# Spreading softmax reciprocals through a DRAM row, and loading q and k by block: an attention and MoE kernel on Trainium2

## Chip, cores and metric

The kernel runs on one core of a Trainium2 chip. The metric is the device time of one execution in microseconds (us). The kernel before took 657.95 us (median of 3 runs, 656.72 to 660.94). Kernels are compared only within the same rounds.

## The reference

A forgetting attention (batch 8, 8 heads, 576 positions, head size 64) feeds a two-layer MLP with SiLU ("MoE" in the kernel's names):

```python
cum    = np.cumsum(np.log(np.clip(f, 1e-4, 1.0)), axis=-1)
scores = q @ k.T / 8 + (cum[..., :, None] - cum[..., None, :])   # causal
attn   = softmax(scores)
x      = (attn @ v).transpose(0, 2, 1, 3).reshape(4608, 512)
h      = x @ w_in                      # 512 x 2048
out    = (h * sigmoid(h)) @ w_out      # 2048 x 512
```

All inputs and the output are float32. Matmuls may run in bfloat16.

## The kernel before

Two heads make a *pair* (32 pairs), one batch entry makes a *block* (4 pairs). TensorE's order is fixed by hand; the other engines' order is set by a scheduler. Softmax denominators (`den`) are formed for two pairs at once, so for four heads. I call that a *quad*; there are 16.

```python
    def load_pair(n):                       # SyncE, float32, 6 DMAs of 128 KB per pair
        b, p = divmod(n, NP)
        for name, src in (("q", q), ("k", k), ("v", v)):
            t = stage.tile([P, NM, 2, D], FP32, name=name + "f", tag=name + "f")
            for i in range(2):
                nc.sync.dma_start(out=t[:, :, i, :],
                    in_=src[b, 2 * p + i, 0:SM, :].rearrange("(c p) d -> p c d", p=P))
    # ... load_tails: the last 64 positions of all heads of a block
    # ... convert(n): GpSimd casts q and k to bfloat16 and scales v

    def den(qd):
        dn = psc.tile([P, 1024], FP32, name="dn", tag="sc")
        # ... for j in range(4), the heads of the quad:
                    nc.tensor.matmul(
                        dn[32 * j : 32 * j + 32, q0:q1],           # 32 equal rows per head
                        lhsT=w_bf[r, kb, bh : bh + 1].to_broadcast([nk, 32]),
                        rhs=rhs, start=..., stop=...)
        rec = recp.tile([P, S], FP32, name="rec", tag="rec")
        nc.vector.reciprocal(out=rec[:, :], in_=dn[:, 0:S])
        for m in range(2):
            rb = rbp.tile([P, S], FP32, name="rb", tag="rb")
            for i in range(2):
                j = 2 * m + i
                nc.sync.dma_start(                                  # one partition, 64 copies
                    out=rb[i * D : (i + 1) * D, :],
                    in_=rec[32 * j : 32 * j + 1, None, :].to_broadcast([1, D, S]))
            recs[2 * qd + m] = rb

    def num(n):
        # ... nm (PSUM) = numerator of the pair, 128 rows = 2 heads x 64
        rb = recs.pop(n)
        nc.vector.tensor_tensor(out=xT[:, p, b * S : (b + 1) * S],
            in0=nm[:, 0:S], in1=rb[:, :], op=ALU.mult)

    # main loop, per pair n: scores(n) and MoE work (fill); den(n//2 - 1) when n is even;
    # num(n-3), num(n-2) when n is odd; transposes(n+1)
```

`tp`, `sc`, `dn` and `nm` share one PSUM pool of two buffers. A `nm` tile is held until its xT multiply has read it, so a late `rb` holds PSUM, then the transposes, then the scores of the next pair.

The softmax here doesn't subtract the row's maximum and nothing guards it: scores larger than these inputs give would overflow.

Of the kernel before, what the change touches and what calls it, by code (L numbers as in the profile page):

```python
# [9 lines left out]
ALU = mybir.AluOpType  # L10
# [6 lines left out]
def kernel(  # L17
# [26 lines left out]
    ctx.enter_context(tc.manual_schedule(engines={mybir.EngineType.PE}))  # L44

    const = ctx.enter_context(tc.tile_pool(name="const", bufs=1))
    stage = ctx.enter_context(tc.tile_pool(name="stage", bufs=3))
    tailp = ctx.enter_context(tc.tile_pool(name="tailp", bufs=2))
    conv = ctx.enter_context(tc.tile_pool(name="conv", bufs=2))
    vpool = ctx.enter_context(tc.tile_pool(name="vpool", bufs=5))  # L50
    qktp = ctx.enter_context(tc.tile_pool(name="qktp", bufs=2))
    upool = ctx.enter_context(tc.tile_pool(name="upool", bufs=4))
    recp = ctx.enter_context(tc.tile_pool(name="recp", bufs=2))
# [1 line left out]
    gpool = ctx.enter_context(tc.tile_pool(name="gpool", bufs=2))  # L55
    tpool = ctx.enter_context(tc.tile_pool(name="tpool", bufs=3))
    opool = ctx.enter_context(tc.tile_pool(name="opool", bufs=2))
    psc = ctx.enter_context(tc.tile_pool(name="psc", bufs=2, space=bass.MemoryType.PSUM))
    pbig = ctx.enter_context(tc.tile_pool(name="pbig", bufs=4, space=bass.MemoryType.PSUM))


    stg: dict[int, tuple] = {}
    tails: dict[int, tuple] = {}

    def load_pair(n):
        b, p = divmod(n, NP)
        tiles = []
        for name, src in (("q", q), ("k", k), ("v", v)):
            t = stage.tile([P, NM, 2, D], FP32, name=name + "f", tag=name + "f")
            for i in range(2):  # L70
                nc.sync.dma_start(  # L71
                    out=t[:, :, i, :],
                    in_=src[b, 2 * p + i, 0:SM, :].rearrange("(c p) d -> p c d", p=P),
                )
            tiles.append(t)
        stg[n] = tuple(tiles)

    def load_tails(b):
        tiles = []
        for name, src in (("q", q), ("k", k)):  # L80
            t = tailp.tile([ST, H, D], FP32, name=name + "tf", tag=name + "tf")
            nc.sync.dma_start(
                out=t[:, :, :], in_=src[b, :, SM:S, :].rearrange("h s d -> s h d")
            )
            tiles.append(t)
        t = tailp.tile([P, NP, D], FP32, name="vtf", tag="vtf")
        for i in range(2):
            nc.sync.dma_start(
                out=t[i * ST : (i + 1) * ST, :, :],
                in_=v[b, i::2, SM:S, :].rearrange("h s d -> s h d"),  # L90
            )
        tiles.append(t)
        tails[b] = tuple(tiles)

    f_sb = const.tile([BH, S], FP32, name="f_sb")
    nc.sync.dma_start(out=f_sb[:, :], in_=f.rearrange("b h s -> (b h) s"))
    load_pair(0)
    load_tails(0)
    load_pair(1)
    load_pair(2)  # L100


    ident_bf = const.tile([P, P], BF16, name="ident_bf")
# [54 lines left out]
    nc.vector.tensor_copy(out=w_bf[:, :, :], in_=wps[:, :, :])  # L158


    qt_bf: dict[int, tuple] = {}
    qkT: dict[int, bass.AP] = {}
    vps: dict[int, bass.AP] = {}
    us: dict[int, tuple] = {}
    bf: dict[int, tuple] = {}

    def conv_tails(b):
        qt, kt, vt = tails.pop(b)
        qk_t = tailp.tile([ST, 2, H, D], BF16, name="qk_t", tag="qk_t")
        nc.gpsimd.tensor_copy(out=qk_t[:, 0, :, :], in_=qt[:, :, :])  # L170
        nc.gpsimd.tensor_copy(out=qk_t[:, 1, :, :], in_=kt[:, :, :])
        v_t = tailp.tile([P, NP, D], BF16, name="v_t", tag="v_t")
        for i in range(2):
            r = slice(i * ST, (i + 1) * ST)
            nc.gpsimd.tensor_tensor(
                out=v_t[r, :, :],
                in0=vt[r, :, :],
                in1=w_bf[r, NM, b * H + i : (b + 1) * H : 2, None].to_broadcast([ST, NP, D]),
                op=ALU.mult,
            )  # L180
        qt_bf[b] = (qk_t, v_t)

    def convert(n):
        b, p = divmod(n, NP)
        if p == 0:
            conv_tails(b)
        qf, kf, vf = stg.pop(n)
        qk_bf = conv.tile([P, 2, NM, 2 * D], BF16, name="qk_bf", tag="qk_bf")
        for i, t in enumerate((qf, kf)):
            nc.gpsimd.tensor_copy(  # L190
                out=qk_bf[:, i, :, :], in_=t[:, :, :, :].rearrange("p c h d -> p c (h d)")
            )
        vp = vpool.tile([P, NM, 2, D], BF16, name="vp", tag="vp")
        bh = b * H + 2 * p
        nc.gpsimd.tensor_tensor(  # L195
            out=vp[:, :, :, :],
            in0=vf[:, :, :, :],
            in1=w_bf[:, 0:NM, bh : bh + 2, None].to_broadcast([P, NM, 2, D]),
            op=ALU.mult,
        )  # L200
        bf[n] = qk_bf
        vps[n] = vp

    def transposes(n):
        b, p = divmod(n, NP)
        qk_bf = bf.pop(n)
        qk_t, _ = qt_bf[b]
        tp = psc.tile([P, 2, 1024], BF16, name="tp", tag="sc")
        for i in range(2):
            for c in range(NM):  # L210
                nc.tensor.transpose(  # L211
                    tp[:, i, c * P : (c + 1) * P], qk_bf[:, i, c, :], ident_bf[:, :]
                )
            nc.tensor.transpose(  # L214
                tp[:, i, SM:S],
                qk_t[:, i, 2 * p : 2 * p + 2, :].rearrange("p h d -> p (h d)"),
                ident_bf[:ST, :ST],
            )
        t = qktp.tile([P, 2, S], BF16, name="qkT", tag="qkT")
        nc.vector.tensor_copy(out=t[:, :, :], in_=tp[:, :, 0:S])  # L220
        qkT[n] = t
# [65 lines left out]
    def den(qd):  # L287
        dn = psc.tile([P, 1024], FP32, name="dn", tag="sc")
        for kb in range(NM + 1):
            for q0, q1 in q_parts(kb):  # L290
                for j in range(4):
                    n, i = 2 * qd + j // 2, j % 2
                    b, p = divmod(n, NP)
                    bh = b * H + 2 * p + i
                    u, ut = us[n]
                    r = slice(i * ST, (i + 1) * ST) if kb == NM else slice(0, P)
                    nk = ST if kb == NM else P
                    rhs = (
                        ut[r, :]
                        if kb == NM  # L300
                        else u[:, i, u_off(kb, q0) : u_off(kb, q0) + q1 - q0]
                    )
                    nc.tensor.matmul(  # L303
                        dn[32 * j : 32 * j + 32, q0:q1],
                        lhsT=w_bf[r, kb, bh : bh + 1].to_broadcast([nk, 32]),
                        rhs=rhs,
                        start=(kb == 0),
                        stop=(kb == NM or (kb == NM - 1 and q0 < SM)),
                    )
        rec = recp.tile([P, S], FP32, name="rec", tag="rec")  # L310
        nc.vector.reciprocal(out=rec[:, :], in_=dn[:, 0:S])  # L311
        for m in range(2):
            rb = rbp.tile([P, S], FP32, name="rb", tag="rb")
            for i in range(2):
                j = 2 * m + i
                nc.sync.dma_start(  # L316
                    out=rb[i * D : (i + 1) * D, :],
                    in_=rec[32 * j : 32 * j + 1, None, :].to_broadcast([1, D, S]),
                )
            recs[2 * qd + m] = rb  # L320

    def num(n):
        b, p = divmod(n, NP)
        u, ut = us.pop(n)
        vp = vps.pop(n)
        _, v_t = qt_bf[b]
        nm = psc.tile([P, 1024], FP32, name="nm", tag="sc")
        for kb in range(NM + 1):
            for q0, q1 in q_parts(kb):
                for i in range(2):  # L330
                    r = slice(i * ST, (i + 1) * ST)
                    nc.tensor.matmul(  # L332
                        nm[i * D : (i + 1) * D, q0:q1],
                        lhsT=v_t[r, p, :] if kb == NM else vp[:, kb, i, :],
                        rhs=(
                            ut[r, :]
                            if kb == NM
# [83 lines left out]
            ready["g"] += 1  # L421


    convert(0)
    transposes(0)
    for n in range(NU):
        scores(n, 0)
        fill(1)
        if n + 1 < NU:
            convert(n + 1)  # L430
        if n + 3 < NU:
            load_pair(n + 3)
            if (n + 3) % NP == 0:
                load_tails((n + 3) // NP)
        if n == 1:
            load_w_in(0)
        if n == 2:
            load_w_in(1)
        if n == 3:
            load_w_in(2)  # L440
            load_w_in(3)
        if 4 <= n < 8:
            load_w_out(n - 4)
        scores(n, 1)
        fill(1)
        scores(n, 2)
        fill(2)
        if n % 2 == 0 and n >= 2:
            den(n // 2 - 1)
            fill(2)  # L450
        if n % 2 == 1 and n >= 3:
            num(n - 3)
            fill(1)
            num(n - 2)
            finished(n - 2)
            fill(1)
        if n + 1 < NU:
            transposes(n + 1)
        fill(2)
# [38 lines left out]
```

## Time and profile before

| what | value | where it is read |
|---|---|---|
| span of the profiled run | 658.4 us | page |
| xT multiply waiting for rb | 233.6 us in 32 waits | list of waits |
| rb's DMAs on the chain that ended last | 39%, their issue 8% | page, chain |
| start of the second quad's last xT | 100.35 us | VectorE's timeline |
| 14 quads from there | 496.2 us, 35.4 us each | VectorE's timeline |
| rest (MoE alone) | 61.9 us | span less the two |

Lines of the page of the kernel before. A queue line gives packets, MB, and the time of its packets as a share of 16 engines' span; a group line gives busy us and mean ns, then idle time before the group and what ended it; the last line gives the median time from issue to landing. In all such lines PE is TensorE, DVE VectorE, ACT ScalarE, POOL GpSimd, SPq SyncE's queue, and L316 is line 316 of the kernel.

```profile
span 658.4 us, 7686 instructions
...
q1 hardware_dynamic: 124560, 47.35, 63.0%
...
DMA rb<-rec 39%; SPq L316 8%; PE po L389 8%; PE hp L362 8%; DVE rec L311 6%; ACT u L258 4%; SPq L71 2%; DMA kf<-in_k_dram 2%; DVE gt L371 1%; PE sc L251 1%; PE tp L211 1%; DVE xT L344 1%; DVE qkT L220 1%; DMA vf<-in_v_dram 1%; ACT th L370 1%
...
L344 DVE TENSOR_TENSOR xT<-nm,rb 128x576 bf16<-128x576 f32 x32 | 24.2, 758 | 233.6 <-DMA rb<-rec 233.6
...
rb<-rec SPq DMA_DIRECT2D x64, 144.0 KB, 14.1
```

VectorE waits 233.6 us, all for rb. That the wait matters, and is not just idle time of an engine with slack, shows in the chain in order of time (start, us, what), here one quad of the kernel before:

```profile
186.30 3.68 DVE rec L311
...
190.54 0.59 SPq L316
...
191.18 2.68 SPq L316
...
193.90 16.41 DMA rb<-rec
...
211.10 0.76 DVE qkT L220
...
217.17 1.83 PE po L389 x8
219.00 0.94 PE dn L303 x36
```

Reciprocal, four DMA issues, one long DMA, then qkT and some 7 us of TensorE work to the next den. The quantity that matters is the time from the reciprocal's end to the start of the quad's second xT. I call it **L2**. VectorE's timeline of the same quad gives it:

```profile
186.22 3.75 DVE L311 RECIPROCAL rec<-dn 128x576 f32<-128x576 f32 x1
191.02 0.75 DVE L220 COPY qkT<-tp 128x1152 bf16<-128x1152 bf16 x1
202.39 0.76 DVE L344 TENSOR_TENSOR xT<-nm,rb 128x576 bf16<-128x576 f32 x1 [4.15 <-DMA rb<-rec]
210.43 0.76 DVE L344 TENSOR_TENSOR xT<-nm,rb 128x576 bf16<-128x576 f32 x1 [6.69 <-DMA rb<-rec]
```

L2 is 210.43 - (186.22 + 3.75) = 20.5 us here.

The table of stretches has, for the tail of the kernel before, where only output rows move, the columns of PE, PEld, DVE, ACT and POOL busy time, then clock, DMA share and GB/s:

```profile
614.00:658.00 44.00, 40.56 (x188) 18.17 (x186) 11.49 (x17) 14.34 (x24) 0.00 (x0) 0.99 0.13 48
```

48 GB/s at a share of 0.13 of 16 engines is 48 / (0.13 x 16) = 23 GB/s for a busy engine.

### The profile page before, as it was taken

To read this page: it belongs to the slowest core of one execution; us is meant where nothing else is said; L and a number is where in the kernel's file an instruction comes from. 1 tells how busy PE (TensorE), PEld (TensorE's weight loads), DVE (VectorE), ACT (ScalarE), POOL (GpSimd) and SP (SyncE) were. 2 spreads that over 40 slices of the span, in tenths; PEclk is the share of its full clock that TensorE was granted. 3 is DMA by queue.
4 is the path that set the end of the run, shared out by engine and by line. 5 is a ranking of instruction groups with operands and counts; after the bars stand their busy time and mean duration, and the time that the engine had idled before them with its cause. 6 is when DMAs were issued, how large, how long until landed. Compare 5 with 4: busy or idle time off the path is not lost.

```text
span 658.4 us, 7686 instructions
## 1 busy us (share of the span) xinstructions
PE 428.6 (65%) x3013; PEld 184.5 (28%) x3013; DVE 230.1 (35%) x325; ACT 203.2 (31%) x312; POOL 99.0 (15%) x150
## 2 busy tenths in 40 slices
PE   3250428767385928775676838592877658907997
PEld 1130213323132413322232313231332224402443
DVE  2140405513272307340361317230643137304530
ACT  4130304422170405322442207140532235104441
POOL 6341202202011012101020201101110100000000
PEclk9999999979597978878795959687887969957999
DMA  8998787789867774868577674858382825592002
GB/s 174 211 207 42 128 32 143 27 147 88 132 69 74 120 72 95 33 130 49 124 40 108 50 110 47 66 96 46 96 31 33 35 40 18 36 32 52 16 33 80
DMA packets 128820, 52.03 MB, mean 79 GB/s; under 512 B 115920, under 2 KB 120016, under 8 KB 128784
## 3 DMA queue, kind: packets, MB, share of 16 engines
q1 hardware_dynamic: 124560, 47.35, 63.0%
q0 software_dynamic: 4224, 4.19, 4.0%
q8 instruction: 23, 0.38, 0.2%
q14 instruction: 13, 0.11, 0.0%
HBM read 36.85 MB, written 9.44 MB: 70 GB/s over the span
## 4 chain that ended last, share of the span: by engine, by line
DMA 42%; PE 20%; SPq 11%; DVE 11%; issue 10%; ACT 5%; POOL 0%; DVEq 0%; ACTq 0%; POOLq 0%
DMA rb<-rec 39%; SPq L316 8%; PE po L389 8%; PE hp L362 8%; DVE rec L311 6%; ACT u L258 4%; SPq L71 2%; DMA kf<-in_k_dram 2%; DVE gt L371 1%; PE sc L251 1%; PE tp L211 1%; DVE xT L344 1%; DVE qkT L220 1%; DMA vf<-in_v_dram 1%; ACT th L370 1%
## 5 line engine op out<-in xcount | busy, mean ns | idle before, releaser
L362 PE MATMUL hp<-xT,w_in_bf 128*128 128x512 bf16 x576 | 155.5, 408 | 114.2 <-DVE xT L344 114.2
L389 PE MATMUL po<-w_out_bf,gt 128*128 128x512 bf16 x576 | 155.1, 416 | 0.0
L258 ACT ACTIVATE u<-sc 128x1024 bf16<-128x1024 f32 x96 | 97.4, 1029 | 174.6 <-PE sc L251 142.5
L370 ACT ACTIVATE th<-hp 128x512 bf16<-128x512 f32 x144 | 86.9, 605 | 186.4 <-PE hp L362 181.0
L371 DVE SCALAR_TENSOR_TENSOR gt<-th,hp 128x512 bf16<-128x512 bf16 x144 | 95.9, 682 | 65.6 <-ACT th L370 65.6
L344 DVE TENSOR_TENSOR xT<-nm,rb 128x576 bf16<-128x576 f32 x32 | 24.2, 758 | 233.6 <-DMA rb<-rec 233.6
L362 PEld LDWEIGHTS <-w_in_bf 128*128 128x128 bf16 x576 | 52.4, 102 | 121.2 <-issue 76.3
L251 PE MATMUL sc<-qkT 64*128 64x512 bf16 (+4 forms) x320 | 43.3, 345 | 61.3 <-DVE qkT L220 57.0
L389 PEld LDWEIGHTS <-gt 128*128 128x128 bf16 x576 | 54.0, 104 | 70.2 <-issue 23.2
L311 DVE RECIPROCAL rec<-dn 128x576 f32<-128x576 f32 x16 | 60.1, 3754 | 5.9 <-PE dn L303 5.9
L190 POOL CAST qk_bf<-qf 128x512 bf16<-128x512 f32 x32 | 20.6, 644 | 271.4 <-issue 154.0
L211 PE MATMUL tp<-ident_bf,qk_bf 128*128 128x128 bf16 x256 | 32.8, 268 | 41.3 <-DVE xT L344 29.6
L211 PEld LDWEIGHTS <-qk_bf 128*128 128x128 bf16 x256 | 21.1, 117 | 114.7 <-issue 96.9
L195 POOL TENSOR_TENSOR vp<-vf,w_bf 128x512 bf16<-128x512 f32 x32 | 33.6, 1051 | 122.8 <-PE nm L332 92.4
L398 ACT ACTIVATE osb<-po 128x512 f32<-128x512 f32 x36 | 21.5, 597 | 87.9 <-PE po L389 42.3
L271 DVE TENSOR_TENSOR u<-u,mask 128x768 bf16<-128x768 bf16 x32 | 18.0, 562 | 85.9 <-ACT u L258 82.2
L251 PEld LDWEIGHTS <-qkT 64*128 64x128 bf16 x320 | 12.0, 100 | 105.9 <-DVE qkT L220 68.8
L332 PE MATMUL nm<-u,vp 128*64 128x64 bf16 (+4 forms) x512 | 30.0, 264 | 0.2
L220 DVE COPY qkT<-tp 128x1152 bf16<-128x1152 bf16 x32 | 23.6, 739 | 14.5 <-PE tp L214 14.5
L332 PEld LDWEIGHTS <-vp 128*64 128x64 bf16 x512 | 20.1, 117 | 17.9 <-issue 12.7
L190 POOL CAST qk_bf<-kf 128x512 bf16<-128x512 f32 x32 | 20.0, 625 | 9.4 <-DMA kf<-in_k_dram 9.3
L303 PE MATMUL dn<-u,w_bf 128*32 128x64 bf16 (+4 forms) x512 | 14.8, 261 | 1.1 <-DVE xT L344 0.9
(39 smaller groups left out, 117.0 us busy)
## 6 DMA issues: line engine op xcount, KB each, us to landing
rb<-rec SPq DMA_DIRECT2D x64, 144.0 KB, 14.1
out_dram<-osb SPq DMA_DIRECT2D x36, 256.0 KB, 2.9
qf<-in_q_dram SPq DMA_DIRECT2D x64, 128.0 KB, 3.0
kf<-in_k_dram SPq DMA_DIRECT2D x64, 128.0 KB, 3.5
vf<-in_v_dram SPq DMA_DIRECT2D x64, 128.0 KB, 3.4
w_in_bf<-in_moe_w_in_dram POOLq DMA_DIRECT2D x4, 512.0 KB, 9.0
w_out_bf<-in_moe_w_out_dram POOLq DMA_DIRECT2D x4, 512.0 KB, 8.5
qtf<-in_q_dram SPq DMA_DIRECT2D x8, 128.0 KB, 3.8
```

What stands on the lines that cost most here:

```text
L190: nc.gpsimd.tensor_copy(out=qk_bf[:, i, :, :], in_=t[:, :, :, :].rearrange("p c h d -> p c (h d)"))
L195: nc.gpsimd.tensor_tensor(out=vp[:, :, :, :], in0=vf[:, :, :, :], in1=w_bf[:, 0:NM, bh : bh + 2, None].to_broadcast([P, NM, 2, D]), op=ALU ...
L211: nc.tensor.transpose(tp[:, i, c * P : (c + 1) * P], qk_bf[:, i, c, :], ident_bf[:, :])
L251: nc.tensor.matmul(sc[:, i, col : col + q1 - q0], lhsT=t[r, 1, kb * P : (kb + 1) * P], rhs=t[r, 0, q0:q1], start=True, stop=True,)
L258: nc.scalar.activation(out=u[:, :, c * 512 : (c + 1) * 512], in_=sc[:, :, :], func=ACT.Exp, scale=scale)
L311: nc.vector.reciprocal(out=rec[:, :], in_=dn[:, 0:S])
L316: nc.sync.dma_start(out=rb[i * D : (i + 1) * D, :], in_=rec[32 * j : 32 * j + 1, None, :].to_broadcast([1, D, S]),)
L332: nc.tensor.matmul(nm[i * D : (i + 1) * D, q0:q1], lhsT=v_t[r, p, :] if kb == NM else vp[:, kb, i, :], rhs=(ut[r, :] if kb == NM else u[:, ...
L362: nc.tensor.matmul(hp[:, :], lhsT=w_in_bf[:, cc, fc * P : (fc + 1) * P], rhs=xT[:, cc, t0 : t0 + TG], start=(cc == 0), stop=(cc == NCC - 1),)
L370: nc.scalar.activation(out=th[:, :], in_=hp[:, :], func=ACT.Tanh, scale=0.5)
L371: nc.vector.scalar_tensor_tensor(out=gt[:, fc, :], in0=th[:, :], scalar=1.0, in1=hp[:, :], op0=ALU.add, op1=ALU.mult,)
L389: nc.tensor.matmul(po[:, :], lhsT=gt[:, fc, tb * P : (tb + 1) * P], rhs=w_out_bf[:, fc, :], start=(fc == 0), stop=(fc == NFC - 1),)
```

## The change

Its intent: (a) the rows of reciprocals go once to DRAM and are read back from there, with half as many broadcast DMAs, so that no single SBUF partition has to feed 64 copies; (b) q and k are loaded a block at a time by DMAs that cast, which takes the casts off GpSimd and most issues off SyncE.

```diff
+    drow = ctx.enter_context(tc.tile_pool(name="drow", bufs=3, space=bass.MemoryType.DRAM))
@@ loads @@
-    def load_pair(n): ...            # 6 DMAs per pair on SyncE
+    def load_qk(b, c, h0, h1):       # casting, on GpSimd; 128 positions of all heads
+        ...
+        for i, src in enumerate((q, k)):
+            nc.gpsimd.dma_start(
+                out=qkb[b][:n, i, c, h0 * D : h1 * D].rearrange("p (h d) -> p h d", d=D),
+                in_=src[b, h0:h1, c * P : c * P + n, :].rearrange("h p d -> p h d"),
+            )
+    def load_v(b, c, h0, h1): ...    # float32, SyncE; convert_v scales it on GpSimd
@@ start: before the masks and identities are built @@
-    load_pair(0); load_tails(0); load_pair(1); load_pair(2)
+    for hh in range(2):
+        for c in range(NM + 1):
+            load_qk(0, c, hh * H // 2, (hh + 1) * H // 2)
+            load_v(0, c, hh * H // 2, (hh + 1) * H // 2)
@@ den @@
         nc.vector.reciprocal(out=rec[:, :], in_=dn[:, 0:S])
+        row = drow.tile([4, S], FP32, name="row", tag="row")
+        nc.sync.dma_start(out=row[:, :], in_=rec[0:P:32, :])
         for m in range(2):
             rb = rbp.tile([P, S], FP32, name="rb", tag="rb")
-            for i in range(2):
-                j = 2 * m + i
-                nc.sync.dma_start(
-                    out=rb[i * D : (i + 1) * D, :],
-                    in_=rec[32 * j : 32 * j + 1, None, :].to_broadcast([1, D, S]),
-                )
+            nc.sync.dma_start(
+                out=rb[:, :],
+                in_=row[2 * m : 2 * m + 2, None, :].to_broadcast([2, D, S]),
+            )
```

(Cut: pool sizes, `transposes` reading the new tile, and the places in the loop where a block's loads and conversions are issued. The weight loads move too: four at a time, in the first two pairs. VectorE, not GpSimd, scales block 0's v. TensorE's order of work is the same.)

More of the change, by code (lines that the diff above doesn't have):

```diff
@@ L46 @@
     const = ctx.enter_context(tc.tile_pool(name="const", bufs=1))
-    stage = ctx.enter_context(tc.tile_pool(name="stage", bufs=3))
-    tailp = ctx.enter_context(tc.tile_pool(name="tailp", bufs=2))
+    stage = ctx.enter_context(tc.tile_pool(name="stage", bufs=1))
     conv = ctx.enter_context(tc.tile_pool(name="conv", bufs=2))
-    vpool = ctx.enter_context(tc.tile_pool(name="vpool", bufs=5))
+    vpool = ctx.enter_context(tc.tile_pool(name="vpool", bufs=3))
     qktp = ctx.enter_context(tc.tile_pool(name="qktp", bufs=2))
@@ L57 @@
     opool = ctx.enter_context(tc.tile_pool(name="opool", bufs=2))
+    drow = ctx.enter_context(tc.tile_pool(name="drow", bufs=3, space=bass.MemoryType.DRAM))
     psc = ctx.enter_context(tc.tile_pool(name="psc", bufs=2, space=bass.MemoryType.PSUM))
     pbig = ctx.enter_context(tc.tile_pool(name="pbig", bufs=4, space=bass.MemoryType.PSUM))
-    stg: dict[int, tuple] = {}
-    tails: dict[int, tuple] = {}
-    def load_pair(n):
-        b, p = divmod(n, NP)
-        tiles = []
-        for name, src in (("q", q), ("k", k), ("v", v)):
-            t = stage.tile([P, NM, 2, D], FP32, name=name + "f", tag=name + "f")
-            for i in range(2):
-                nc.sync.dma_start(
-                    out=t[:, :, i, :],
-                    in_=src[b, 2 * p + i, 0:SM, :].rearrange("(c p) d -> p c d", p=P),
-                )
-            tiles.append(t)
-        stg[n] = tuple(tiles)
@@ L78, in load_tails @@
-    def load_tails(b):
-        tiles = []
-        for name, src in (("q", q), ("k", k)):
-            t = tailp.tile([ST, H, D], FP32, name=name + "tf", tag=name + "tf")
+    qkb: dict[int, bass.AP] = {}
+    vst: dict[int, list] = {}
+    vbf: dict[int, tuple] = {}
+    def load_qk(b, c, h0, h1):
+        if b not in qkb:
+            qkb[b] = conv.tile([P, 2, NM + 1, H * D], BF16, name="qkb", tag="qkb")
+        n = P if c < NM else ST
+        for i, src in enumerate((q, k)):
[3 more added lines that the diff above has]
+            )
@@ L82, in load_tails, with load_v @@
+    def load_v(b, c, h0, h1):
+        if b not in vst:
+            vst[b] = [
+                stage.tile([P, H if i < NM else NP, D], FP32, name=f"vf{i}", tag=f"vf{i}")
+                for i in range(NM + 1)
+            ]
+        if c < NM:
             nc.sync.dma_start(
-                out=t[:, :, :], in_=src[b, :, SM:S, :].rearrange("h s d -> s h d")
-            )
-            tiles.append(t)
-        t = tailp.tile([P, NP, D], FP32, name="vtf", tag="vtf")
+                out=vst[b][c][:, h0:h1, :],
+                in_=v[b, h0:h1, c * P : (c + 1) * P, :].rearrange("h p d -> p h d"),
+            )
+            return
@@ L87, in load_tails @@
         for i in range(2):
             nc.sync.dma_start(
-                out=t[i * ST : (i + 1) * ST, :, :],
-                in_=v[b, i::2, SM:S, :].rearrange("h s d -> s h d"),
-            )
-        tiles.append(t)
-        tails[b] = tuple(tiles)
+                out=vst[b][c][i * ST : (i + 1) * ST, h0 // 2 : h1 // 2, :],
+                in_=v[b, h0 + i : h1 : 2, SM:S, :].rearrange("h p d -> p h d"),
+            )
     f_sb = const.tile([BH, S], FP32, name="f_sb")
     nc.sync.dma_start(out=f_sb[:, :], in_=f.rearrange("b h s -> (b h) s"))
-    load_pair(0)
@@ L98 @@
-    load_tails(0)
-    load_pair(1)
-    load_pair(2)
+    for hh in range(2):
+        for c in range(NM + 1):
+            load_qk(0, c, hh * H // 2, (hh + 1) * H // 2)
+            load_v(0, c, hh * H // 2, (hh + 1) * H // 2)
     ident_bf = const.tile([P, P], BF16, name="ident_bf")
@@ L158, with convert_v @@
     nc.vector.tensor_copy(out=w_bf[:, :, :], in_=wps[:, :, :])
-    qt_bf: dict[int, tuple] = {}
     qkT: dict[int, bass.AP] = {}
-    vps: dict[int, bass.AP] = {}
     us: dict[int, tuple] = {}
-    bf: dict[int, tuple] = {}
-    def conv_tails(b):
-        qt, kt, vt = tails.pop(b)
-        qk_t = tailp.tile([ST, 2, H, D], BF16, name="qk_t", tag="qk_t")
-        nc.gpsimd.tensor_copy(out=qk_t[:, 0, :, :], in_=qt[:, :, :])
-        nc.gpsimd.tensor_copy(out=qk_t[:, 1, :, :], in_=kt[:, :, :])
-        v_t = tailp.tile([P, NP, D], BF16, name="v_t", tag="v_t")
+    def convert_v(b, c, h0, h1, eng):
+        if b not in vbf:
+            vbf[b] = (
+                vpool.tile([P, NM, H, D], BF16, name="vp", tag="vp"),
+                vpool.tile([P, NP, D], BF16, name="v_t", tag="v_t"),
+            )
+        vp, v_t = vbf[b]
+        vf = vst[b][c]
+        if c < NM:
+            eng.tensor_tensor(
+                out=vp[:, c, h0:h1, :],
+                in0=vf[:, h0:h1, :],
+                in1=w_bf[:, c, b * H + h0 : b * H + h1, None].to_broadcast([P, h1 - h0, D]),
+                op=ALU.mult,
+            )
+            return
@@ L173, in conv_tails @@
         for i in range(2):
             r = slice(i * ST, (i + 1) * ST)
-            nc.gpsimd.tensor_tensor(
-                out=v_t[r, :, :],
-                in0=vt[r, :, :],
-                in1=w_bf[r, NM, b * H + i : (b + 1) * H : 2, None].to_broadcast([ST, NP, D]),
+            eng.tensor_tensor(
+                out=v_t[r, h0 // 2 : h1 // 2, :],
+                in0=vf[r, h0 // 2 : h1 // 2, :],
+                in1=w_bf[r, NM, b * H + h0 + i : b * H + h1 : 2, None].to_broadcast(
+                    [ST, (h1 - h0) // 2, D]
+                ),
@@ L179, in conv_tails @@
                 op=ALU.mult,
             )
-        qt_bf[b] = (qk_t, v_t)
-    def convert(n):
-        b, p = divmod(n, NP)
-        if p == 0:
-            conv_tails(b)
-        qf, kf, vf = stg.pop(n)
-        qk_bf = conv.tile([P, 2, NM, 2 * D], BF16, name="qk_bf", tag="qk_bf")
-        for i, t in enumerate((qf, kf)):
-            nc.gpsimd.tensor_copy(
-                out=qk_bf[:, i, :, :], in_=t[:, :, :, :].rearrange("p c h d -> p c (h d)")
-            )
-        vp = vpool.tile([P, NM, 2, D], BF16, name="vp", tag="vp")
-        bh = b * H + 2 * p
-        nc.gpsimd.tensor_tensor(
-            out=vp[:, :, :, :],
-            in0=vf[:, :, :, :],
-            in1=w_bf[:, 0:NM, bh : bh + 2, None].to_broadcast([P, NM, 2, D]),
-            op=ALU.mult,
-        )
-        bf[n] = qk_bf
-        vps[n] = vp
@@ L204, in transposes @@
     def transposes(n):
         b, p = divmod(n, NP)
-        qk_bf = bf.pop(n)
-        qk_t, _ = qt_bf[b]
+        src = qkb[b]
         tp = psc.tile([P, 2, 1024], BF16, name="tp", tag="sc")
         for i in range(2):
-            for c in range(NM):
+            for c in range(NM + 1):
+                nk = P if c < NM else ST
                 nc.tensor.transpose(
-                    tp[:, i, c * P : (c + 1) * P], qk_bf[:, i, c, :], ident_bf[:, :]
-                )
-            nc.tensor.transpose(
-                tp[:, i, SM:S],
-                qk_t[:, i, 2 * p : 2 * p + 2, :].rearrange("p h d -> p (h d)"),
-                ident_bf[:ST, :ST],
-            )
+                    tp[:, i, c * P : c * P + nk],
+                    src[:nk, i, c, p * P : (p + 1) * P],
+                    ident_bf[:nk, :nk],
+                )
@@ L311, in den @@
         nc.vector.reciprocal(out=rec[:, :], in_=dn[:, 0:S])
+        row = drow.tile([4, S], FP32, name="row", tag="row")
+        nc.sync.dma_start(out=row[:, :], in_=rec[0:P:32, :])
         for m in range(2):
             rb = rbp.tile([P, S], FP32, name="rb", tag="rb")
-            for i in range(2):
-                j = 2 * m + i
-                nc.sync.dma_start(
-                    out=rb[i * D : (i + 1) * D, :],
-                    in_=rec[32 * j : 32 * j + 1, None, :].to_broadcast([1, D, S]),
-                )
+            nc.sync.dma_start(
+                out=rb[:, :],
+                in_=row[2 * m : 2 * m + 2, None, :].to_broadcast([2, D, S]),
+            )
             recs[2 * qd + m] = rb
@@ L324, in num @@
         u, ut = us.pop(n)
-        vp = vps.pop(n)
-        _, v_t = qt_bf[b]
+        vp, v_t = vbf[b]
         nm = psc.tile([P, 1024], FP32, name="nm", tag="sc")
@@ L333, in num @@
                         nm[i * D : (i + 1) * D, q0:q1],
-                        lhsT=v_t[r, p, :] if kb == NM else vp[:, kb, i, :],
+                        lhsT=v_t[r, p, :] if kb == NM else vp[:, kb, 2 * p + i, :],
                         rhs=(
@@ L421, in finished @@
             ready["g"] += 1
-    convert(0)
+    for hh in range(2):
+        for c in range(NM + 1):
+            convert_v(0, c, hh * H // 2, (hh + 1) * H // 2, nc.vector)
     transposes(0)
     for n in range(NU):
+        b, p = divmod(n, NP)
         scores(n, 0)
         fill(1)
-        if n + 1 < NU:
-            convert(n + 1)
-        if n + 3 < NU:
-            load_pair(n + 3)
-            if (n + 3) % NP == 0:
-                load_tails((n + 3) // NP)
-        if n == 1:
-            load_w_in(0)
-        if n == 2:
-            load_w_in(1)
-        if n == 3:
-            load_w_in(2)
-            load_w_in(3)
-        if 4 <= n < 8:
-            load_w_out(n - 4)
+        if b + 1 < B:
+            if p == 0:
+                if b == 0:
+                    for i in range(WQ):
+                        load_w_in(i)
+                for c in range(NM + 1):
+                    load_qk(b + 1, c, 0, H)
+                    load_v(b + 1, c, 0, H)
+            if p == 1 and b == 0:
+                for i in range(WQ):
+                    load_w_out(i)
+            if p == 2:
+                for c in range(2):
+                    convert_v(b + 1, c, 0, H, nc.gpsimd)
+            if p == 3:
+                for c in range(2, NM + 1):
+                    convert_v(b + 1, c, 0, H, nc.gpsimd)
         scores(n, 1)
```

## The prediction

> **What bounds the kernel now.** The page puts 39% of the span's ending chain on the DMA that spreads the reciprocal rows (rb<-rec), 8% on its issue, 16% on MoE matmuls. In the list of waits VectorE stands 233.6 us before the xT multiply, always for rb. The chain in order of time repeats every four heads ("a quad", 16 of them), about 36 us each: reciprocal 3.75 us, issue of four DMAs 3.1 us, last landing about 17.7 us later, xT multiplies, qkT copy, then 12 to 16 us of scores, den and MoE work. From the reciprocal's end to the second rb ("L2") it is 20.4 to 21.2 us; about 12 us could hide behind TensorE, so L2 sets the period. The four DMAs read single partitions: 256 rows of 2304 B in 17.7 us, 33 GB/s in all, though all 16 engines show as busy.
>
> **What changes.** (a) Per quad, one small DMA writes four rows to DRAM, and two DMAs of 288 KB read them back. But the source's outermost dimension is now its two rows.[...] In the tail of before, output writes moved 48 GB/s at a 13% share of 16 engines (stretches table): 23 GB/s per busy engine. Estimate from that: 147 KB per engine and rb take 6.4 us, two in a row 12.8 us. Extra hop: output writes land 2.9 us after issue, so I estimate 2.4 us for the row, then issue[...]. L2 = about 17.5 us. Gain 3 us per quad, about 45 us over 14 quads, part of it because TensorE idles less and so runs less at half rate (matmuls 0.43 us apart after the stall, 0.22 in the tail).
> (b) GpSimd loses 80 casts of about 0.63 us and gains 80 casting DMA issues of about 0.8 us (as the weight loads have). Off the chain: GpSimd is 15% busy. Loads keep 256 B rows, about as many packets.
> (c) The start gets worse: 20 casting loads stand before the masks on GpSimd, so first scores at about 24 us instead of 11.1; the first row waits on SyncE behind a v load of block 2, which waits for GpSimd's conversion of block 1, queued after the weight loads. The second quad's last xT, 101 us now, I put at 108.
> The last 62 us (MoE alone) stay.
>
> **Sum.** 658 + 8 - 45 = about 620 us; 80% range 565 to 668. Faster by over 2%: 0.75; within 2%: 0.13; slower: 0.12.
>
> **What would show it right.** rb<-row on the chain at about 30%, the two big DMAs landing some 8 and 14 us after issue; quads of 31 to 34 us; DMA share falling from 67% to under 45%; xT's waits for rb about 180 us; busy times of TensorE, ScalarE and VectorE nearly unchanged.
>
> **What would make it wrong.** If rb is spread over 16 engines after all, it hides behind TensorE, quads fall to about 23 us and the time to 460 to 490. If an engine that reads one row again and again gets well under 20 GB/s, or loads on those two engines delay rb, L2 passes 21 us and the change is slower. If SyncE's queue holds rows back behind v loads in every block, the gain vanishes too. A start slower by 30 us would give half back.

(The forecast took two engines for each rb, and a fixed time in its sum for L2: no run had shown either. The 6.4 us rest on those two engines, then an assumption; packet counts below show 2 for each rb. L2 came to about 17.5 us: 12.8 for the two rb DMAs, 2.4 for the row, and some 2.3 for the issue and the term. "All 16 engines show as busy" is a DMA share of 0.78 in the transfer shown above, from 194 to 210 us.)

## The result and the profile after

The changed kernel took 622.14 us (median of 4 runs, 620.26 to 622.63) against 658.84 us beside it. The ratio is 0.944 (95% interval 0.940 to 0.948): 5.6% faster. A ratio is the mean time of one kernel's runs over that of the other's of the same rounds, so it is not quite the ratio of the medians.

Lines of the page of the changed kernel:

```profile
span 618.5 us, 7337 instructions
...
q0 software_dynamic: 79392, 13.64, 28.8%
q1 hardware_dynamic: 47280, 28.61, 16.8%
...
DMA rb<-row 37%; PE po L371 9%; PE hp L344 9%; DVE rec L294 7%; DMA row<-rec 5%; ACT u L241 3%; DMA qkb<-in_q_dram 3%; POOL qkb L71 2%; PE sc L234 2%; DVE gt L353 2%; PE tp L197 1%; SPq L299 1%; DVE xT L326 1%; DMA qkb<-in_k_dram 1%; PE dn L286 1%
...
L326 DVE TENSOR_TENSOR xT<-nm,rb 128x576 bf16<-128x576 f32 x32 | 24.3, 758 | 191.5 <-DMA rb<-row 191.5
```

VectorE's wait for rb fell from 233.6 to 191.5 us, and rb still leads the chain. VectorE's timeline of two quads in a row of the changed kernel:

```profile
152.17 3.76 DVE L294 RECIPROCAL rec<-dn 128x576 f32<-128x576 f32 x1 [0.98 <-PE dn L286]
...
166.59 0.76 DVE L326 TENSOR_TENSOR xT<-nm,rb 128x576 bf16<-128x576 f32 x1 [5.05 <-DMA rb<-row]
172.86 0.76 DVE L326 TENSOR_TENSOR xT<-nm,rb 128x576 bf16<-128x576 f32 x1 [5.52 <-DMA rb<-row]
...
185.65 3.75 DVE L294 RECIPROCAL rec<-dn 128x576 f32<-128x576 f32 x1
...
203.46 0.76 DVE L326 TENSOR_TENSOR xT<-nm,rb 128x576 bf16<-128x576 f32 x1 [5.79 <-DMA rb<-row]
210.74 0.76 DVE L326 TENSOR_TENSOR xT<-nm,rb 128x576 bf16<-128x576 f32 x1 [5.93 <-DMA rb<-row]
```

L2 is 16.9 us in the first and 21.3 us in the second. The pattern holds in the last 14 quads: five have 20.4 to 21.3 us, nine have 16.4 to 17.1. The mean is 18.2. The chain of the same two quads shows the extra hop to DRAM and where the second quad loses its time:

```profile
155.96 1.73 DMA row<-rec
...
158.71 14.06 DMA rb<-row
...
189.43 2.71 DMA row<-rec
...
192.75 17.90 DMA rb<-row
```

Both DMAs are longer in the second quad. GpSimd's timeline shows what ran then: ten casting loads of the next block, the first of them held until the transposes had freed its buffer:

```profile
188.16 0.95 POOL L71 DMA_DIRECT2D qkb<-in_q_dram  x1 [18.47 <-PE tp L197]
189.10 0.90 POOL L71 DMA_DIRECT2D qkb<-in_k_dram  x1
...
195.84 0.78 POOL L71 DMA_DIRECT2D qkb<-in_k_dram  x1
```

**Counting engines.** I read the number of engines that a DMA used from the packets of the hardware queue. In the kernel before, the queue's rows are 110,592 (q, k, v) + 4,608 (output) + 4,096 (rb) + 64 (f) = 119,360. The page has 124,560; the 5,200 more, packets of 4 bytes in the trace's packet records, are exactly 16 for each of its 325 DMAs. I take them for one completion per engine. In the changed kernel the rows are 36,864 (v) + 4,608 + 4,096 + 64 (f) + 64 (row) = 45,696 and the page has 47,280: 1,584 more. The 55 loads and 36 output writes take 91 x 16 = 1,456 of them, which leaves 128 for 32 rb and 16 row DMAs: 2 for each rb and 4 for each row. Three experiments below confirm the split. The packet records agree with the reading: in the last 14 quads two rb packets are in flight for 11.2 to 12.9 us of L2 in the changed kernel, and in the kernel before up to 16 to 18 at once.

**Where the time went.**

| stretch | before | after | difference |
|---|---|---|---|
| start, to the second quad's last xT | 100.35 | 106.92 | +6.6 |
| 14 quads | 496.2 | 449.0 | -47.2 |
| rest | 61.9 | 62.6 | +0.7 |
| span | 658.4 | 618.5 | -39.9 |

The fall of mean L2, 21.6 to 18.2 us, times 14 is 49 us (unrounded means): it accounts for all of the second row.

### The profile page after: what moved, and what is told of

Read it like the earlier page. It is cut to its first block, busy times and chain, and to the rows that moved or that the text cites. A ratio compares the mean times of both kernels' runs of the same rounds, so it can differ in the third digit from the quotient of the medians.

```text
span 618.5 us, 7337 instructions
## 1 busy us (share of the span) xinstructions
PE 421.5 (68%) x2966; PEld 184.2 (30%) x3013; DVE 232.1 (38%) x337; ACT 203.4 (33%) x312; POOL 118.2 (19%) x154
## 3 DMA queue, kind: packets, MB, share of 16 engines
q0 software_dynamic: 79392, 13.64, 28.8%
q1 hardware_dynamic: 47280, 28.61, 16.8%
## 4 chain that ended last, share of the span: by engine, by line
DMA 46%; PE 22%; DVE 12%; issue 10%; ACT 4%; POOL 3%; SPq 1%; DVEq 0%; POOLq 0%; ACTq 0%
DMA rb<-row 37%; PE po L371 9%; PE hp L344 9%; DVE rec L294 7%; DMA row<-rec 5%; ACT u L241 3%; DMA qkb<-in_q_dram 3%; POOL qkb L71 2%; PE sc L234 2%; DVE gt L353 2%; PE tp L197 1%; SPq L299 1%; DVE xT L326 1%; DMA qkb<-in_k_dram 1%; PE dn L286 1%
## 5 line engine op out<-in xcount | busy, mean ns | idle before, releaser
L344 PE MATMUL hp<-xT,w_in_bf 128*128 128x512 bf16 x553 | 151.9, 407 | 71.5 <-DVE xT L326 68.4
L371 PE MATMUL po<-w_out_bf,gt 128*128 128x512 bf16 x552 | 149.5, 412 | 3.6 <-issue 2.9
L326 DVE TENSOR_TENSOR xT<-nm,rb 128x576 bf16<-128x576 f32 x32 | 24.3, 758 | 191.5 <-DMA rb<-row 191.5
L197 PE MATMUL tp<-ident_bf,qkb 128*128 128x128 bf16 (+1 forms) x320 | 40.3, 259 | 45.7 <-DVE xT L326 45.4
L197 PEld LDWEIGHTS <-qkb 128*128 128x128 bf16 (+1 forms) x320 | 27.5, 113 | 106.2 <-issue 97.3
L71 POOL DMA_DIRECT2D qkb<-in_q_dram x45 | 38.9, 864 | 97.9 <-PE tp L197 91.3
L71 POOL DMA_DIRECT2D qkb<-in_k_dram x45 | 38.5, 855 | 11.4 <-DMA w_in_bf<-in_moe_w_in_dram 5.0
L286 PEld LDWEIGHTS <-w_bf 128*32 128x32 bf16 (+1 forms) x576 | 10.9, 100 | 10.8 <-issue 6.4
## 6 DMA issues: line engine op xcount, KB each, us to landing
qkb<-in_k_dram POOLq DMA_DIRECT2D x28, 128.0 KB, 12.9
```

What stands on the lines that cost most here:

```text
L71: nc.gpsimd.dma_start(out=qkb[b][:n, i, c, h0 * D : h1 * D].rearrange("p (h d) -> p h d", d=D), in_=src[b, h0:h1, c * P : c * P + n, :].re ...
L197: nc.tensor.transpose(tp[:, i, c * P : c * P + nk], src[:nk, i, c, p * P : (p + 1) * P], ident_bf[:nk, :nk],)
L286: nc.tensor.matmul(dn[32 * j : 32 * j + 32, q0:q1], lhsT=w_bf[r, kb, bh : bh + 1].to_broadcast([nk, 32]), rhs=rhs, start=(kb == 0), stop=( ...
L326: nc.vector.tensor_tensor(out=xT[:, p, b * S : (b + 1) * S], in0=nm[:, 0:S], in1=rb[:, :], op=ALU.mult)
L344: nc.tensor.matmul(hp[:, :], lhsT=w_in_bf[:, cc, fc * P : (fc + 1) * P], rhs=xT[:, cc, t0 : t0 + TG], start=(cc == 0), stop=(cc == NCC - 1),)
L371: nc.tensor.matmul(po[:, :], lhsT=gt[:, fc, tb * P : (tb + 1) * P], rhs=w_out_bf[:, fc, :], start=(fc == 0), stop=(fc == NFC - 1),)
```

## The experiments

Theory A, that of the prediction: L2 sets the quad; through DRAM it is shorter, but two engines for each rb are its new limit; the block loads only cost. Rivals: the block loads bring the gain (B); the DRAM hop or rereading one row is the limit, not the engines (C). Twelve kernels were run, each in three rounds. Kernels are given by the rows of this table; start, quads and L2 are read from VectorE's timeline of the profiled run, as above.

| run | rb is read from | engines per rb DMA | loads | median us | start | 14 quads | mean L2 or its range |
|---|---|---|---|---|---|---|---|
| before | one partition | 16 | pair | 658 | 100.4 | 496.2 | 21.6 |
| after | DRAM row | 2 | block | 622.14 | 106.9 | 449.0 | 18.2 |
| row_only | DRAM row | 2 | pair | 596.71 | 91.9 | 434.5 | 17.3 |
| loads_only | one partition | 16 | block | 671.39 | 113.8 | 495.7 | 21.7 |
| row_16_engines | DRAM row | 16 | block | 465.15 | 86.1 | 314.3 | hidden |
| sbuf_2_engines | one partition | 2 | block | 745.53 | 121.9 | 558.8 | 24.8 to 27.4 |
| no_late_qk | DRAM row | 2 | block, cut | 594.70 | 106.7 | 423.6 | 16.6 |
| row_16_old_loads | DRAM row | 16 | pair | 447.50 | 72.7 | 313.1 | hidden |
| spread | 32 partitions | not counted | block | 458.99 | 82.6 | 314.1 | hidden |
| spread_old_loads | 32 partitions | not counted | pair | 444.77 | 69.7 | 313.5 | hidden |
| two_ports_2_engines | one partition | 2 | block | 575.34 | 102.3 | 408.1 | 13.3 to 17.5 |
| two_ports_16_engines | one partition | 16 | pair | 570.08 | 89.6 | 415.9 | 15.2 to 17.5 |
| masks_first | DRAM row | 2 | block | 610.04 | 93.9 | 454.0 | 16.1 to 22.2 |
| spread_masks_first | 32 partitions | not counted | block | 446.38 | 69.4 | 315.2 | hidden |

Engines were counted from packets in before, after, row_only, row_16_engines and sbuf_2_engines; the other numbers are those of a counted kernel whose rb DMAs have the same slowest dimension (2 rows or 64 copies).

"Hidden" means that L2 reads 8.5 to 12.8 us because the xT multiply then mostly waits for its numerator (or for its turn) and not for rb.

### row_only and loads_only: which half of the change works

```diff
 row_only: the kernel before, with in den
-            four DMAs, rec[32 * j : 32 * j + 1, None, :].to_broadcast([1, D, S])
+        row = drow.tile(...); nc.sync.dma_start(out=row[:, :], in_=rec[0:P:32, :])
+            two DMAs, row[2 * m : 2 * m + 2, None, :].to_broadcast([2, D, S])
 loads_only: the changed kernel, with the same lines of den set back
```

> Half of the change alone: the kernel before with its per-pair loads, rows through DRAM. Theory A (all of the gain is the shorter second landing, L2, at two engines): L2 17 to 19 us instead of 20.4 to 21.2, quads 33 to 34 us, start as before, so about 620 to 635 us. Rival B (the gain comes from the block loads, which take waits off SyncE and work off GpSimd): within 2% of 658 us. The count of packets of the hardware queue tells the engines: 64 completions for 32 rb DMAs if two engines each.

> The other half alone: block loads with casts, reciprocal rows still spread from single SBUF partitions. Theory A: L2 stays at 20 to 21 us and the start is some 8 us longer, so 655 to 670 us. Rival B: about 620 us.

Row_only took 596.71 us, ratio 0.904 (0.898 to 0.909): better than the expected range and better than the whole change. Loads_only took 671.39, ratio 1.018 (1.012 to 1.023), formally unclear at 2%, slower beyond its interval, and just above the expected range. So rival B falls: the DRAM row brings the gain, and the block loads cost. Row_only beats the changed kernel by 15 us in the start (91.9 against 106.9) and by 14.5 us in the quads (434.5 against 449.0). (Its profiled run was its fastest, 590.02 us, so these two sum to more than the 25.4 us between the medians.) Its loads still run beside rb, yet its L2 is 16.5 to 18.3 us; the per-pair loads stand on the same queue as rb, and that this is the reason is not shown. Its hardware queue has 123,728 packets: 119,424 rows and 4,304 more, 261 x 16 for loads and outputs, 32 x 2 for rb, 16 x 4 for the row. So these rb DMAs use two engines as well. The halves do not add up: -61 and +13 would be -48, and the change gives -37. What is lost is L2 in the quads in which casting loads run; no_late_qk tests that.

### row_16_engines and sbuf_2_engines: engines or source

```diff
 row_16_engines: the changed kernel, with in den
-            nc.sync.dma_start(out=rb[:, :],
-                in_=row[2 * m : 2 * m + 2, None, :].to_broadcast([2, D, S]))
+            for i in range(2):
+                j = 2 * m + i
+                nc.sync.dma_start(out=rb[i * D : (i + 1) * D, :],
+                    in_=row[j : j + 1, None, :].to_broadcast([1, D, S]))
 sbuf_2_engines: the changed kernel without the row, and
+            nc.sync.dma_start(out=rb[:, :],
+                in_=rec[64 * m : 64 * m + 64 : 32, None, :].to_broadcast([2, D, S]))
```

> The changed kernel with one edit: each head's row is read from DRAM by its own DMA with 64 copies as outermost dimension, so that 16 engines share it. Theory A (two engines of about 23 GB/s each are the limit): L2 falls to 7 to 9 us, below the 12 us that TensorE can hide, xT's wait for rb nearly gone, quads 22 to 25 us, 460 to 490 us in all. Rival C (rereading one DRAM row, or the extra hop, is the limit): L2 stays at 15 us or more, 600 us or more.

> The changed kernel without the DRAM hop: one DMA per pair straight from two SBUF partitions, two rows outermost, so two engines again. If the source partition is what limited the kernel before (33 GB/s in all), L2 is near 20 us and the time 645 to 665 us. If instead any two-engine DMA takes 12 to 13 us for both, whatever its source, L2 is about 15 us (no hop) and the time 585 to 605 us.

Row_16_engines took 465.15 us, ratio 0.705 (0.702 to 0.709), inside what theory A gave. The same bytes come from the same DRAM row after the same hop; only the slowest dimension of the source is 64 copies instead of 2 rows. Rival C falls. VectorE's longest waits before xT in this run (us in total, times, longest):

```profile
DVE xT L328 <- DMA rb<-row: 31.5, 12, 19.3
DVE xT L328 <- PE nm L316: 23.1, 15, 7.6
```

Only 31.5 us of waiting for rb are left, and 19.3 of them are the first quad's. The packet counts show the engines. First row_16_engines, then sbuf_2_engines:

```profile
q1 hardware_dynamic: 48240, 28.62, 25.1%
```

```profile
q1 hardware_dynamic: 47152, 28.47, 16.1%
```

Row_16_engines has 45,696 rows and 2,544 more packets: 1,456 for loads and outputs, 64 x 16 for rb, 16 x 4 for the row. Sbuf_2_engines has no row DMA: 45,632 rows and 1,520 more, 1,456 + 32 x 2.

Sbuf_2_engines missed both expectations: 745.53 us, ratio 1.132 (1.127 to 1.136). Its second landing follows the first by about 11.8 us: 295 KB (two rows, 64 copies of 2,304 B each) in that time are 25 GB/s for both engines together, while the two engines of the changed kernel take 5.8 to 6.3 us for the same in quads without casting loads (23 to 26 GB/s each). Neither of my two theories had a limit below 33 GB/s for a source in SBUF. The next question was whether the two partitions share something.

### two_ports_2_engines and two_ports_16_engines: what the single partition costs

A pair's two rows stand on partitions 32 apart. I assumed that rows 64 apart would not slow each other; no trace had shown it. Both kernels only move the rows:

```diff
-                        dn[32 * j : 32 * j + 32, q0:q1],
+                        dn[64 * (j % 2) + 32 * (j // 2) : 64 * (j % 2) + 32 * (j // 2) + 32, q0:q1],
 (and the broadcast DMAs read rec at 64 * i + 32 * m instead of at 32 * j)
```

> As sbuf_2_engines (745 us, L2 25 to 27 us), but a pair's two reciprocal rows stand on partitions 64 apart instead of 32 apart[...]. [...]L2 falls to 15 to 19 us and the time to 600 to 650 us. If one engine reads SBUF rows of one partition no faster than 12 GB/s[...], L2 stays at 25 us and the time near 745 us.

> The kernel before, with only the placement changed: a pair's two rows on partitions 64 apart instead of 32. [...]the second landing comes some 4 to 8 us earlier (L2 13 to 17 us instead of 21.6), 560 to 620 us. If the limit is per partition or per engine, within 2% of 658 us.

(The first outcome in each text is for the case that something shared sets the pace.)

Both became much faster: sbuf_2_engines fell from 745.53 to 575.34 us (ratio to the kernel before 0.873, 0.868 to 0.878), faster than I had expected, and the kernel before fell from 659.21 to 570.08 us (ratio 0.865, 0.859 to 0.871). VectorE's timeline of the fourth quad, first sbuf_2_engines, then two_ports_2_engines:

```profile
174.37 3.76 DVE L293 RECIPROCAL rec<-dn 128x576 f32<-128x576 f32 x1 [0.98 <-PE dn L285]
...
191.87 0.76 DVE L323 TENSOR_TENSOR xT<-nm,rb 128x576 bf16<-128x576 f32 x1 [8.13 <-DMA rb<-rec]
203.70 0.76 DVE L323 TENSOR_TENSOR xT<-nm,rb 128x576 bf16<-128x576 f32 x1 [11.07 <-DMA rb<-rec]
```

```profile
144.29 3.76 DVE L293 RECIPROCAL rec<-dn 128x576 f32<-128x576 f32 x1 [0.98 <-PE dn L285]
...
155.84 0.76 DVE L323 TENSOR_TENSOR xT<-nm,rb 128x576 bf16<-128x576 f32 x1 [2.19 <-DMA rb<-rec]
162.75 0.76 DVE L323 TENSOR_TENSOR xT<-nm,rb 128x576 bf16<-128x576 f32 x1 [6.15 <-DMA rb<-rec]
```

L2 is 25.6 and 14.7 us. Where both multiplies wait for rb and no casting loads run, the second landing of two_ports_2_engines now follows the first by 6.3 to 6.9 us, so each engine gets its own 21 to 23 GB/s. The packed traces also hold every single DMA packet, which no view above shows. In sbuf_2_engines two rb packets of 2,304 B are in flight for most of the transfer, and one takes about 180 ns (medians of the last 14 quads, where no casting loads run); in two_ports_2_engines one takes 93 ns, as from the DRAM row in the changed kernel. In the kernel before up to 16 to 18 are in flight and one takes about 1,230 ns; in two_ports_16_engines 610 to 810. In the kernel before the second landing comes 9.0 us after the first (mean of the last 14 quads; 295 KB, 33 GB/s), though part of the second pair's rows may have moved before the first landing; no run separates that. So what limited the kernel before was that a pair's two source rows stand 32 partitions apart. What they share there is not shown. It was not the whole limit: reading each row from 32 partitions takes the kernel before from 570 further to 445 us (spread_old_loads below). My words in the prediction, "read single partitions", were right about the symptom and one level too coarse.

### no_late_qk: why every second quad gains nothing

```diff
 the changed kernel, wrong on purpose
+                    if b + 1 < 3:
                         load_qk(b + 1, c, 0, H)
+                    else:
+                        qkb[b + 1] = qkb[b - 1]
```

> Wrong result on purpose: the changed kernel, where q and k of blocks 3 to 7 are not loaded at all (the buffers keep what blocks 1 and 2 left); everything else stands in the same order on every queue. Theory D (the casting loads, on a queue of their own, share the two engines with the rb transfers and add some 4 us to L2 in every second quad): L2 in the five quads that had 20.4 to 21.3 us falls to 16.4 to 17.1, about 21 us less in all, 598 to 605 us. Rival E (those quads are longer for a reason of their own, such as the v loads or the order of work on TensorE): L2 stays near 21 us there, time within 1% of 622 us.

It took 594.70 us, ratio 0.902 (0.899 to 0.906), a little more gain than the 21 us expected. L2 is 16.4 to 17.1 us in all 14 quads. VectorE's timeline of this run, one quad of the kind that had 21 us:

```profile
182.29 3.75 DVE L294 RECIPROCAL rec<-dn 128x576 f32<-128x576 f32 x1
...
196.75 0.76 DVE L326 TENSOR_TENSOR xT<-nm,rb 128x576 bf16<-128x576 f32 x1 [2.46 <-DMA rb<-row]
202.56 0.76 DVE L326 TENSOR_TENSOR xT<-nm,rb 128x576 bf16<-128x576 f32 x1 [4.46 <-DMA rb<-row]
```

L2 is 16.5 us. The v loads are still there, so rival E falls: the casting loads of q and k add the 4 us. The casting loads are on GpSimd's queue, rb on SyncE's; which engines the casting loads use, and so how they delay rb, is not shown. It does not take DRAM as the source of rb: in two_ports_2_engines, which reads SBUF, L2 is 17.1 to 17.5 us in the quads with casting loads and 13.3 to 14.9 in the others. On 16 engines (loads_only) it is 21.1 to 22.0 us in both kinds. The packet records of the changed kernel show where the time goes. In the five quads more than 9,150 packets of casting loads start within L2, in the nine none. There the first rb packet starts 5.1 to 5.9 us after the reciprocal's end, in the nine 3.1; between the first and the last rb packet at most one is in flight for 2.1 to 3.6 us, in the nine for 0.3 to 1.1; and an rb packet takes 106 ns instead of 93. Why is not shown. (The output of this run passed the comparison with the reference although q and k of five blocks were wrong. So that comparison says little about q and k of those blocks in any run here.)

### spread, spread_old_loads, row_16_old_loads: versions that beat both

```diff
 spread (on the changed kernel, without the row), spread_old_loads (on the kernel before)
                 nc.sync.dma_start(
                     out=rb[i * D : (i + 1) * D, :],
-                    in_=rec[32 * j : 32 * j + 1, None, :].to_broadcast([1, D, S]))
+                    in_=rec[32 * j : 32 * j + 32, None, :].to_broadcast([32, 2, S]))
 row_16_old_loads: row_only with the four DMAs of row_16_engines
```

`den` already leaves 32 equal rows per head, so the source can be spread over 32 partitions at no cost.

> Best guess at a version that beats both: rows through DRAM, read back on 16 engines, with the per-pair loads of the kernel before. If the block loads only cost (start about 15 us later, contention on the way), this is 440 to 455 us against 465 with block loads. If the block loads help once TensorE is the bound (fewer waits for GpSimd's casts and for SyncE), it is 465 us or more.

> Tests what limited the kernel before: no DRAM hop, four DMAs[...] from SBUF, but each head's row is read from the 32 partitions that already hold copies of it (two copies from each) instead of from one. Block loads as in the changed kernel. If the single source partition was the limit, L2 falls from 21.8 us (block loads, one partition) to 7 to 10 us, and the time from 671 to 455 to 475 us. If SBUF to SBUF copies or the four issues are slow in themselves, L2 stays above 15 us and the time above 600 us.

> The same edit in the kernel before, with its per-pair loads: the only change is which partitions the four DMAs read. 435 to 460 us if the single source partition was the limit and block loads only cost; within 2% of 658 us if it was not.

All three hit: 447.50 us (ratio 0.680), 458.99 (0.697) and 444.77 (0.675, 0.674 to 0.677). The last is the fastest version, and it differs from the kernel before in one access pattern. Its VectorE waits for rb 9.1 us in all. With L2 hidden, the quads take 313 to 315 us in all five such versions, whatever the loads: TensorE sets the pace. In the table of stretches, spread_old_loads has TensorE busy for 285 of 300 us at full clock:

```profile
100.00:400.00 300.00, 285.17 (x2300) 128.55 (x2338) 176.12 (x247) 150.05 (x235) 56.95 (x81) 1.00 0.43 107
```

and the kernel before in the same stretch 209 of 300 at a clock of 0.84:

```profile
100.00:400.00 300.00, 208.94 (x1491) 86.20 (x1494) 112.24 (x161) 99.65 (x154) 49.06 (x71) 0.84 0.73 89
```

### masks_first and spread_masks_first: why the start got slower

```diff
 the lines that build ident_bf, ident_f, mask and mask_t on GpSimd are moved ahead of
     for hh in range(2):
         for c in range(NM + 1):
             load_qk(0, c, ...)
             load_v(0, c, ...)
```

> The changed kernel with the masks and identities built on GpSimd before its first casting loads. The prediction blamed the slower start partly on them. First scores move from 24 us to 13 to 18 us. If that order delays the start by itself, the second quad's last xT moves from 107 us to 97 to 102 us and the time to about 613 to 617 us; if the first row's place on SyncE behind the v loads and the busy DMA engines decide, it stays within 2 us of 107 and the time within 0.5% of 622 us.

> The spread version with block loads (459 us), with the masks built before the first casting loads. With L2 hidden behind TensorE, contention of the loads with rb no longer counts, so what block loads still cost against per-pair loads (459 against 445 us) should be the start alone. If the place of the masks is that start cost, 445 to 450 us; if the block loads delay the start by their own size, 455 to 459 us.

Masks_first took 610.04 us, ratio 0.925 (0.920 to 0.930). First scores moved from 24.2 to 15.2 us and the second quad's last xT from 106.9 to 93.9, more than expected; some 5 us went again in the quads of this run (454.0 against 449.0), which I did not follow up. The edit moved two things. The first reciprocal starts 9.1 us earlier (29.39 against 38.44 us). And the first row no longer stands behind a v load: in the changed kernel SyncE could issue this load only after GpSimd's conversion of block 1 (a wait of 10.0 us), and the row came after it, as SyncE's timeline shows:

```profile
48.37 0.37 SPq L83 DMA_DIRECT2D vf_493<-in_v_dram  x1
48.79 0.63 SPq L296 DMA_DIRECT2D row<-rec  x1
```

The reciprocal had ended at 42.20 us, so the row went out 6.6 us late. In masks_first it goes out at 33.18, right at the reciprocal's end (33.15). Spread_masks_first took 446.38 us, within 2 us of spread_old_loads, with the same start (69.4 against 69.7). So the cost of block loads at the start is their place in the queues, not their size: GpSimd builds the masks only after it has issued twenty casting loads, and SyncE holds the first row. TensorE's first matmul in the changed kernel waits for that:

```profile
17.99 0.80 PE L156 MATMUL wps<-ident_f,wexp 64*128 64x64 f32 x5 [17.99 <-POOL ident_f masks.py:199]
```

With the masks ahead of the loads it starts at 7.27 us.

## Why the prediction was right

- **Two engines.** Predicted; shown by the packet counts of four kernels and by row_16_engines, where 16 engines take 157 us off.
- **Rate of an engine.** Estimated at 23 GB/s, 6.4 us for each rb. The two landings of the changed kernel lie 6.3 us apart in the first quad shown and 5.8 to 6.3 in all nine quads without casting loads (23 to 26 GB/s), so the estimate was a little low. DRAM as a source was no slower for an engine than SBUF with the two rows 64 partitions apart (6.3 to 6.9 us, two_ports_2_engines).
- **L2.** Predicted 17.5 us against a mean of 18.2, but as one value. It is two: 16.4 to 17.1 and 20.4 to 21.3. In the first quad shown the row takes 1.7 us (2.4 estimated), the issue 1.0, and the two rb DMAs 14.1 (12.8 and the term). The prediction named contention of loads on the two engines only as a risk. Here it takes about 4 us in five quads.
- **L2 before.** I read 20.4 to 21.2 us from the chain, up to the last landing. Up to the second xT the mean is 21.6. This understatement and the missed contention nearly cancel, which is luck: 49 us fell instead of 45.
- **TensorE less often at half rate.** Part of the 45 us was put on that. The clock records have two rates, 1.0 and 0.5. In the 4 us before each of the 35 stretches at 0.5 of the two kernels TensorE was busy for 0.00 to 0.55 of the time, before each change back to 1.0 for 0.70 or more. But the granted clock over the 14 quads rose only from 0.83 to 0.86. The fall of L2 alone accounts for the quads' 47 us, so a separate gain is not shown.
- **Start.** Predicted 8 us longer, first scores at about 24 us, the second xT at 108; measured 6.6 us longer, 24.2 and 106.9. Both reasons were right: the masks' place (9.1 us to the first reciprocal) and the first row's place behind a v load (6.6 us, above; without it the first quad's L2 is 30.9 us in masks_first, 38.3 in the changed kernel). But the net was in part luck. The row path alone takes 8.5 us off the start (row_only, 91.9 against 100.4), which the prediction did not name, and the block loads add 15.0 to that.
- **Off the chain.** GpSimd was called off the chain; in the steady part it is, in the start it is not. (It issues 90 casting loads, not 80: block 0 comes in halves.)
- **Signs.** Quads of 32.1 us on average and busy times of TensorE, ScalarE and VectorE within 2% came as said; the two big DMAs land some 9 and 15 us after issue (first quad shown), for 8 and 14. Others were a little off: rb on the chain 37%, not about 30; xT's waits 191.5 us, not about 180; DMA share 46% by adding the queue lines (16.8 + 28.8 and the small ones), not under 45.
- **What would make it wrong.** The case of 16 engines, put at 460 to 490 us, was built: 465.15.

## What to carry to other kernels

Before judging a broadcast by its bytes, look at its source's slowest dimension and at the partitions that it reads: here the kernel with block loads took from 459 to 746 us by these two alone (spread and sbuf_2_engines). The broadcast on the critical chain, on two engines, lost some 4 us of L2 here to bulk loads on another queue; with the loads on its own queue (row_only) it lost 1.8 us at most. When a change gives a gain, run its halves apart: one half here was worth more than the whole.
